# A hand-ordered two-part SSM kernel: another order of all engines' work, other buffer slots, and six groups of output stores issued by SyncE

## The chip, the cores and the metric

The kernel runs on one core of one Trainium2 chip. The metric is the device time of one execution in microseconds (us). A core has five engines that work side by side, each through its own list of instructions in order: TensorE (PE in the profile, its weight loads PEld), VectorE (DVE), ScalarE (ACT), GpSimd (POOL) and SyncE (SP). SP computes nothing; it issues transfers. POOL issues transfers as well. [...]

## The reference

Two independent parts share the launch, and their results are put side by side.

```python
def _A_ref(q, k, v, shift_k, ssm_k, ssm_D):          # S = 2048, D = 1024
    k_shift = sum of 4 shifted copies of k, each times a column of shift_k
    kv = k_shift * v
    y = irfft(rfft(kv padded to 2S) * rfft(ssm_k padded to 2S))[:S] + kv * ssm_D
    return q * y

def _B_ref(x, Lambda_re, Lambda_im, B_re, B_im, C_re, C_im, log_dt, Dskip):
    Lam_bar = exp(dt * Lam);  B_bar = ((Lam_bar - 1.0) / Lam)[:, None] * Bmat
    Bu = x @ B_bar.T                                  # complex
    for t in range(L): h = Lam_bar * h + Bu[t]        # complex state, kept for all t
    y = 2.0 * (hseq @ Cmat.T).real + x * Dskip
    return y

return concatenate([_A_ref(...), _B_ref(...)], axis=-1)
```

## The kernel before

The long string `ORDER` is the program: each word is one task, and words run from left to right, which fixes the order on every engine. A word is `task.args:slots`; `p0` to `p7` are the eight PSUM banks, `a..`, `b..`, `m..` and `w..` are numbered SBUF buffers. A task that takes a slot waits until the former user of the slot is done. Nothing is tiled by a loop; the order was written out by a planner beforehand.

Part B. `bl`/`cl` load blocks of B and C (256 KB each, SP), `bT`/`cT` transpose them on PE into PSUM (8 matmuls), `bc`/`cc` copy them to SBUF (ACT; `bc` for imaginary blocks 0 to 3 on DVE). `cx` loads blocks of C already transposed. `ld_par` loads four small vectors, `par_T`, `p32`, `exp1`, `dve2`, `tabA1`, `sin1`, `tabA2`, `par_rest`, `eo`, `z1`, `stt`, `z2` make the rotation tables out of them, `dd` the diagonal and the decay table. Then the sequence goes in 16 chunks of 128 steps: `x.i` loads the chunk, `U.i.jp` (32 matmuls) multiplies it with B, `ue` evicts; on DVE `r1`, `r2` rotate, `rc` adds the carry, `sc` scans, `cm`, `ca` make the next carry, `r3`, `r4` rotate back; `y.i.dh.part` multiplies with C, `ye` evicts and `yst` stores (chunk 15 is stored by `ye` itself from SP, L547).

Part A is a long convolution as a two-stage Fourier transform. `kp`, `vp` load k and v, `kvm`, `kv1`, `kv2`, `kva` make kv on DVE; `am` is its first stage (PE), `ae` evicts, `ast` stores to DRAM. `hl`, `hT`, `hc`, `hm`, `he`, `hst` do the same for the filter. Stage two, for 32 groups: `lw`, `lh`, `lk` load constants and both spectra, `sh`, `sk` multiply, `she`, `ske` evict, `sw` swaps halves by DMA, `pr` multiplies on DVE, `sa` goes back, `sae` evicts, `vst` stores. `vl` loads the result, `a3` is the last stage, `a3e` evicts, `qm` multiplies with q (loaded by `qp`), `op` stores four pieces (L786). `wb`, `wbe` broadcast the four taps, which `ld_w` loads.

`wm.n` is n matmuls on zeros whose result nobody reads. POOL issues `ld_w`, `ld_G`, `ld_F`, `ld_sd`, `ast`, `hst`, `vst`, `yst` and `op`; all loads and `sw` go through SP, which waits in order for slots and for one of eight semaphores: a ninth load is issued when the first has landed.

```python
spd = nc.sync.dma_start
gpd = nc.gpsimd.dma_start
```

Of the kernel before, what the change touches and what calls it, by code (L numbers as in the profile page):

```python
# [51 lines left out]
wbe.4 bT.0.1:p5 wbe.6 wb.0:p6 bc.0.1 wbe.5 wb.1:p7 wb.2:p0 wbe.0 wb.3:p1 wbe.2 wbe.3 ld_par wbe.7 wm.13:p3 bT.2.1:p3 wbe.1 bl.7.1:b5 bc.2.1 wm.3:p2
bT.0.0:p2 bl.2.0:b6 bc.0.0 bl.1.1:b7 wm.3:p5 bT.1.0:p5 bl.5.1:b8 bc.1.0 vp.0:a2 wm.14:p6 par_T:p6 p32 wm.5:p0 bT.7.1:p0 exp1 bc.7.1 dve2 wm.3:p1
bT.2.0:p1 x.0:b9 dve3 tabA1:a3a4a5a6 wm.3:p4 bT.1.1:p4 bc.2.0 bl.5.0:b10 wm.3:p7 bT.5.1:p7 exp2 cl.2.1:b0 bc.5.1 cl.2.0:b1 sm_pre sin1 kp.0 tabA2 sin0
bl.7.0:b2 bl.3.1:b3 wm.30:p3 bT.5.0:p3 bc.5.0 par_rest hl.2.1:a7 wm.3:p2 cT.2.1:p2 bl.4.1:b4 wm.3:p5 cT.2.0:p5 sin2 cc.2.1 bc.1.1 dd cc.2.0 wm.15:p6
# [798 lines left out]
```

## Time and profile before

| | us |
|---|---|
| median of 11 runs | 376.54 |
| lowest and highest run | 374.06, 378.57 |
| the profiled execution, own time | 377.71 |
| its span, first to last instruction | 375.8 |
| busy: PE, DVE, ACT, POOL | 356.9, 324.6, 278.3, 71.7 |
| mean granted TensorE clock | 0.986 |

A line of the timeline gives the start, the duration of a merged group, engine, source line, operation, output and inputs, the count, and in brackets the idle time before it and what ended it. A line of the windows gives the stretch, its length and the busy time (count) of PE, PEld, DVE, ACT and POOL, then the granted clock, the DMA share and GB/s.

### The profile page before, as it was taken

What the parts mean: (1) busy time and instruction counts of PE and PEld (TensorE: products, weight loads), DVE (VectorE), ACT (ScalarE), POOL (GpSimd) and SP (SyncE); (2) the same over time, 40 slices, a digit from 0 to 9 for tenths busy, and PEclk for the clock granted to TensorE, in tenths of its full rate; (3) what the DMA queues carried; (4) which work ended last, traced back from release to release, by engine and by line L of the source; (5) the groups of instructions that cost most, each with busy time, mean ns of one, the idle gap of its engine ahead of it and who ended that gap; (6) DMA issues with size and microseconds to landing.
All of it is one profiled execution on the core that took longest, in us unless ns stands there. A gap on an engine that the chain in (4) does not pass through costs nothing.

```text
span 375.8 us, 9490 instructions
## 1 busy us (share of the span) xinstructions
PE 356.9 (95%) x3821; PEld 250.1 (67%) x3851; DVE 324.6 (86%) x335; ACT 278.3 (74%) x519; POOL 71.7 (19%) x124
## 2 busy tenths in 40 slices
PE   7998699999999999999999999999999999999991
PEld 5777699996587787895855456457764445575640
DVE  2299989999999999999999999359999999159990
ACT  4599889989649875976558996788799975175541
POOL 4000003222331252221000110111010111124551
PEclk9999699999999999999999999999999999999997
DMA  8999999958989997589899899999797999799953
GB/s 214 275 295 284 334 255 274 262 181 222 263 280 198 331 232 219 164 292 340 272 270 275 281 280 328 289 268 331 198 329 216 281 271 329 259 399 402 326 150 95
DMA packets 61643, 101.14 MB, mean 269 GB/s; under 512 B 31536, under 2 KB 33872, under 8 KB 61599
## 3 DMA queue, kind: packets, MB, share of 16 engines
q1 hardware_dynamic: 51502, 67.13, 65.3%
q0 software_dynamic: 10096, 33.40, 26.3%
q8 instruction: 30, 0.49, 0.5%
q14 instruction: 15, 0.11, 0.1%
HBM read 52.27 MB, written 33.55 MB: 228 GB/s over the span
## 4 chain that ended last, share of the span: by engine, by line
PE 74%; ACT 9%; DMA 7%; DVE 4%; issue 2%; POOL 1%; POOLq 0%; ACTq 0%; DVEq 0%
PE ps_u L460 27%; PE ps_y L529 24%; PE ps_a L692 6%; PE ps_a L732 6%; PE ps_a L661 3%; DMA vv<-Vs 3%; DMA out_dram<-ot 3%; PE ps_t L424 2%; PE ps_y L534 2%; PE ps_t L641 2%; ACT hab L702 1%; ACT x L711 1%; PE ps_a L611 1%; DMA hk<-in_A_shift_k_dram 1%; POOL out_dram L786 1%
## 5 line engine op out<-in xcount | busy, mean ns | idle before, releaser
L460 PEld LDWEIGHTS <-BT 128*128 128x128 bf16 x2048 | 119.0, 99 | 9.7 <-issue 4.1
L460 PE MATMUL ps_u<-xT,BT 128*128 128x128 bf16 x2048 | 124.4, 221 | 0.9 <-DVE BT L435 0.6
L529 PE MATMUL ps_y<-CT,h 128*128 128x512 bf16 x488 | 122.8, 379 | 2.1 <-DVE h L488 0.8
L529 PEld LDWEIGHTS <-h 128*128 128x128 bf16 x512 | 45.1, 98 | 47.1 <-issue 1.9
L507 DVE TENSOR_TENSOR_SCAN h<-rtab,h 128x1024 bf16<-128x1024 f32 (+1 forms) x34 | 72.3, 2155 | 0.3
L462 ACT CAST u<-ps_u 128x512 bf16<-128x512 f32 x64 | 39.9, 635 | 31.4 <-PE ps_u L460 30.3
L545 ACT CAST yo<-ps_y 128x512 bf16<-128x512 f32 x32 | 19.5, 614 | 36.0 <-PE ps_y L529 35.7
L723 DVE TENSOR_TENSOR hab<-x,hab 128x2048 bf16<-128x2048 bf16 x32 | 37.9, 1218 | 4.5 <-ACT x L711 4.5
L479 DVE TENSOR_TENSOR mt<-u,Z 128x4096 bf16<-128x4096 bf16 x15 | 34.2, 2283 | 8.9 <-ACT u L462 8.9
L702 ACT CAST hab<-ps_a 128x512 bf16<-128x512 f32 x64 | 36.2, 666 | 4.2 <-PE ps_a L692 2.9
L488 DVE TENSOR_TENSOR h<-mt 128x2048 bf16<-128x2048 bf16 (+1 forms) x34 | 39.0, 1155 | 0.2
L741 ACT CAST vsb<-ps_a 128x512 bf16<-128x512 f32 x64 | 35.0, 650 | 5.7 <-PE ps_a L732 4.7
L711 ACT CAST x<-ps_a 128x512 bf16<-128x512 f32 x64 | 36.8, 683 | 1.5 <-DVE hab L723 0.8
L669 ACT CAST ysbh<-ps_a 128x512 bf16<-128x512 f32 x64 | 35.2, 660 | 0.2 <-PE ps_a L661 0.2
L479 DVE TENSOR_TENSOR mt<-h,Z 128x4096 bf16<-128x4096 bf16 x15 | 34.3, 2287 | 0.1
L622 ACT CAST ysb<-ps_a 128x512 bf16<-128x512 f32 x64 | 34.3, 674 | 0.0
L732 PE MATMUL ps_a<-hab,wts 128*128 128x512 bf16 x122 | 31.2, 379 | 0.2
L582 DVE TENSOR_TENSOR mt<-kring,wbc 128x4096 bf16<-128x4096 bf16 (+3 forms) x16 | 29.9, 1882 | 0.0
L627 POOL DMA_DIRECT2D Ys_kv<-ysb x16 | 11.5, 718 | 90.4 <-ACT ysb L622 90.4
L534 PE MATMUL ps_y<-Dd,xT 128*128 128x128 bf16 x128 | 28.1, 219 | 0.3 <-issue 0.2
L675 POOL DMA_DIRECT2D Ys_h<-ysbh x32 | 22.0, 693 | 30.2 <-ACT ysbh L669 29.4
L745 POOL DMA_DIRECT2D Vs<-vsb x16 | 8.5, 533 | 87.7 <-ACT vsb L741 87.7
(113 smaller groups left out, 403.4 us busy)
## 6 DMA issues: line engine op xcount, KB each, us to landing
Ys_kv<-ysb POOLq DMA_DIRECT2D x16, 512.0 KB, 4.7
Ys_h<-ysbh POOLq DMA_DIRECT2D x32, 256.0 KB, 4.9
l2h<-Ys_h SPq DMA_DIRECT2D x16, 512.0 KB, 4.8
hab<-hab SPq DMA_DIRECT2D x64, 128.0 KB, 4.5
l2k<-Ys_kv SPq DMA_DIRECT2D x16, 512.0 KB, 5.6
Vs<-vsb POOLq DMA_DIRECT2D x16, 512.0 KB, 5.1
vv<-Vs SPq DMA_DIRECT2D x16, 512.0 KB, 11.1
v<-in_A_v_dram SPq DMA_DIRECT2D x32, 128.0 KB, 4.9
```

What stands on the lines that cost most here:

```text
L460: nc.tensor.matmul(pu[:, w, jl, :], BT[:, 2 * jp + jl, w, d, :], xT[:, d, :], start=(d == 0), stop=(d == ND - 1))
L462: E["ue"] = lambda i, jp: nc.scalar.copy(st["u", i][:, :, 2 * jp:2 * jp + 2, :], st.pop(("pu", i, jp))[:])
L479: nc.vector.tensor_mul(m4[:].rearrange("p (a b) w -> p a (b w)", a=2), s_, win(Z, h))
L488: nc.vector.tensor_add(dst[:].rearrange("p a j t -> p a (j t)")[:, :, jw], mv[:, :, 0, jw], mv[:, :, 1, jw])
L507: nc.vector.tensor_tensor_scan(gf, rt1[:, jw], gf, 0.0, ALU.mult, ALU.add)
L529: nc.tensor.matmul(py[:], h[:, 1 - w, j, :], CT[:, j, w, dh * 512:(dh + 1) * 512], start=(j == 0 and w == 0), stop=(j == NJ - 1 and w == 1))
L534: nc.tensor.matmul(py[:, dl * P:(dl + 1) * P], st["xT", i][:, d, :], Dd[:, d, :], start=False, stop=False)
L669: nc.scalar.copy(st["yh", qd, n4][:, :, w, :], st.pop(("pa", qd, n4, w))[:].rearrange("p (c d) -> p c d", c=2))
L702: nc.scalar.copy(st["hab", g][:, 0, cols], pt[:])
L711: nc.scalar.copy(st["x16", g][:, w * 512:(w + 1) * 512], st.pop(("ps", "l2k", g, w))[:])
L723: nc.vector.tensor_mul(hab[:], st.pop(("x16", g))[:].unsqueeze(1).to_broadcast([P, 2, D]), hab[:])
L732: nc.tensor.matmul(pt[:], st["w", gq][:, gi, 1 + a, :], hab[:, a, w * 512:(w + 1) * 512], start=(a == 0), stop=(a == 1))
```

## The change

The words of `ORDER` are put in another order and given other slots. The tasks are the same but for `wm`: 205 zero matmuls in place of 194, at other places. `dd` stands after `stt` and no longer ahead of `kvm.0`; `kvm.2` stands ahead of `kva.0`; `vp.0` is issued behind `hl.0.0`. A new entry `late` of the settings names `op.3`, `yst.12`, `yst.13`, `yst.14`, `op.0` and `op.1`: these stores are issued by SP instead of POOL. `ldw` is 0, so `ld_w` stays on POOL.

```diff
-CFG = {'kr': 8, 'bdve': 4, 'K4': 13, 'kq': 2, 'tabct': 0, 'swsp': 1, 'th': (15,), 'actsw': ()}
+CFG = {'kr': 8, 'bdve': 4, 'K4': 13, 'kq': 2, 'tabct': 0, 'swsp': 1, 'ldw': 0, 'th': (15,), 'actsw': (), 'late': (('op', 3), ('yst', 12), ('yst', 13), ('yst', 14), ('op', 0), ('op', 1))}
...
-ld_w:a0a1 bl.6.1:b0 bl.0.1:b1 kp.-2 ld_G ld_sd ld_F bl.2.1:b2 bl.0.0:b3 wm.22:p0 bT.6.1:p0 wm.5:p1 wb.4:p1 bc.6.1 wb.5:p2 bl.1.0:b4 wb.6:p3 wb.7:p4
-wbe.4 bT.0.1:p5 wbe.6 wb.0:p6 bc.0.1 wbe.5 wb.1:p7 wb.2:p0 wbe.0 wb.3:p1 wbe.2 wbe.3 ld_par wbe.7 wm.13:p3 bT.2.1:p3 wbe.1 bl.7.1:b5 bc.2.1 wm.3:p2
-bT.0.0:p2 bl.2.0:b6 bc.0.0 bl.1.1:b7 wm.3:p5 bT.1.0:p5 bl.5.1:b8 bc.1.0 vp.0:a2 wm.14:p6 par_T:p6 p32 wm.5:p0 bT.7.1:p0 exp1 bc.7.1 dve2 wm.3:p1
-bT.2.0:p1 x.0:b9 dve3 tabA1:a3a4a5a6 wm.3:p4 bT.1.1:p4 bc.2.0 bl.5.0:b10 wm.3:p7 bT.5.1:p7 exp2 cl.2.1:b0 bc.5.1 cl.2.0:b1 sm_pre sin1 kp.0 tabA2 sin0
-bl.7.0:b2 bl.3.1:b3 wm.30:p3 bT.5.0:p3 bc.5.0 par_rest hl.2.1:a7 wm.3:p2 cT.2.1:p2 bl.4.1:b4 wm.3:p5 cT.2.0:p5 sin2 cc.2.1 bc.1.1 dd cc.2.0 wm.15:p6
-U.0.0:p6a8 kp.1 eo cl.1.1:b5 kvm.0:m0 bT.3.1:p0 cl.0.0:b6 bT.7.0:p1 bl.4.0:b7 hl.0.0:a9 wm.10:p7 bT.4.1:p7 bc.3.1 kvm.1:m1 bc.4.1 vp.1:a10 bc.7.0
-wm.23:p3 cT.1.1:p3 kv1.0 ue.0.0 wm.3:p4 cT.0.0:p4 bl.3.0:b8 cc.1.1 kv1.1 hl.0.1:a11 wm.3:p2 bT.4.0:p2 lw.2:w0 cc.0.0 kv2.0:b10 cl.3.1:b0 bc.4.0
-kv2.1:b1 kva.0 z1 kva.1 kvm.2:m0 cl.0.1:b3 wm.30:p5 am.0.0:p5p0p7p1 am.0.1:p6p3p4p2 bl.6.0:b2 x.1:b4 ae.0.0.2:a12 kvm.3:m1 hl.3.0:a0 ae.0.1.3
-bT.3.0:p7 lw.1:w1 ae.0.0.3 hT.0.0:p2 hl.3.1:a1 bc.3.0 hT.0.1:p1 hl.2.0:a2 cl.3.0:b5 hc.0.0:b6 U.0.1:p7 kv1.2 cx.5.0 hc.0.1:b7 hd.0 kv2.2:b10 lw.0:w2
-ae.0.1.2 cT.0.1:p2 kv1.3 ue.0.1 U.0.2:p1 lw.4:w3 ast.0.1 cc.0.1 kva.2 x.3:b1 kv2.3:b8 bT.6.0:p4 ue.0.2 stt cT.3.1:p7 bc.6.0 hT.0.2:p2 x.2:b3 hT.0.3:p1
-cc.3.1 U.0.3:p4 hl.1.0:a9 hc.0.2:b2 hc.0.3:b0 U.1.0:p7a11 cx.5.1 ue.0.3 kva.3 z2 r1.0:m0 hT.2.0:p2 hl.1.1:a10 ue.1.0 U.1.1:p1 ae.0.0.0:a12 ae.0.0.1
...
-y.11.0.1 she.28.0:a6 pr.31 sw.29 she.28.1 y.11.0.2 ske.29.0:b8 r3.12:m0 ske.29.1 y.11.0.3 sw.28 sa.27.0:p5 ye.11.0:b6 sa.27.1:p3 sae.27.0 pr.30
-sa.31.0:p6 sae.27.1 sa.31.1:p1 y.10.1.0:p2 qp.2:a3 cm.12 vst.13 r4.12 sa.30.0:p4 sa.30.1:p0 pr.29 sae.30.0:a11 y.10.1.1 sae.30.1 qp.7:a10 sae.31.0
-pr.28 y.10.1.2 sae.31.1 sa.29.0:p7 ca.12 vst.15 rc.13 sa.28.0:p5 sc.13.0 sa.28.1:p3 sae.28.0:a8 sa.29.1:p4 sae.28.1 y.12.0.0:p0 sae.29.0 sae.29.1
-y.12.0.1 qp.4:a7 sc.13.1 vst.14 U.14.0:p6a18 r3.13:m1 y.10.1.3 qp.5:a16 ue.14.0 y.12.0.2 ye.10.1 y.12.0.3 cm.13 yst.10 r4.13 y.12.1.0:p1 ye.12.0:b10
-ca.13 y.12.1.1 vl.6:a1a2 y.12.1.2 vl.3:a0a6 y.12.1.3 y.11.1.0:p5 ye.12.1 vl.7:a15a13 y.11.1.1 yst.12 vl.2:a11a12 y.11.1.2 y.11.1.3 U.14.1:p3 ye.11.1
-yst.11 a3.6.0:p7p4 ue.14.1 a3.6.1:p6p2 U.14.2:p0 a3e.6.0.0:a8 vl.4:a4a17 a3e.6.0.1 a3e.6.1.1 a3e.6.1.0 U.14.3:p1 ue.14.2 qm.6 op.6 a3.3.0:p5p3 ue.14.3
-a3.3.1:p7p4 y.13.0.0:p2 a3e.3.0.0:a1 vl.5:a2a14 r1.14:m0 a3e.3.1.1 a3e.3.1.0 U.15.0:p6a0 a3e.3.0.1 qm.3 a3.7.0:p0p1 ue.15.0 a3.7.1:p5p4 y.13.0.1
-a3e.7.0.0:a6 vl.0:a18a15 r2.14:a13 op.3 a3e.7.1.0 a3e.7.0.1 y.13.0.2 rc.14 a3e.7.1.1 sc.14.1 a3.2.0:p7p3 a3.2.1:p6p0 a3e.2.0.0:a9 y.13.0.3 vl.1:a11a12
-a3e.2.1.1 a3e.2.1.0 y.13.1.0:p5 sc.14.0 a3e.2.0.1 ye.13.0:b8 y.13.1.1 y.13.1.2 qm.2 y.13.1.3 U.15.1:p1 cm.14 r3.14:m1 ye.13.1 op.2 a3.4.0:p4p7 ue.15.1
-a3.4.1:p0p6 ca.14 U.15.2:p3 a3e.4.0.0:a8 qm.7 yst.13 a3e.4.1.1 a3e.4.1.0 r1.15.0:m0 qp.0:a5 a3e.4.0.1 a3.5.0:p2p5 ue.15.2 a3.5.1:p1p4 r4.14 U.15.3:p6
-a3e.5.0.0:a3 a3e.5.1.1 a3e.5.0.1 qm.4 a3e.5.1.0 y.14.0.0:p0 ue.15.3 r2.15.0:a4 r1.15.1 y.14.0.1 y.14.0.2 rc.15.0 qm.5 y.14.0.3 op.7 sc.15.1.0
-y.14.1.0:p7 ye.14.0:b3 r2.15.1 y.14.1.1 sc.15.0.0 op.4 y.14.1.2 qp.1:a17 rc.15.1 r3.15.0:m1 y.14.1.3 sc.15.0.1 a3.0.0:p3p2 ye.14.1 a3.0.1:p4p5
-a3.1.0:p1p6 a3e.0.0.0:a1 a3.1.1:p0p7 a3e.0.1.0 r4.15.0 a3e.0.0.1 sc.15.1.1 op.5 y.15.0.0:p3 a3e.0.1.1 a3e.1.0.0:a10 qm.0 y.15.0.1 a3e.1.1.0 a3e.1.1.1
-a3e.1.0.1 y.15.1.0:p4 r3.15.1 y.15.1.1 r4.15.1 qm.1 yst.14 y.15.0.2 y.15.0.3 y.15.1.2 ye.15.0:b4 op.0 y.15.1.3 ye.15.1 op.1 yst.15
...
+ld_w:a0a1 bl.0.1:b0 kp.-2 ld_G ld_F ld_sd bl.2.1:b1 bl.7.1:b2 bl.0.0:b3 wm.22:p0 bT.0.1:p0 bc.0.1 wm.23:p1 wb.4:p1 wb.0:p2 wbe.4 wb.5:p3 wb.6:p4 wbe.0
+wb.7:p5 wbe.6 wb.1:p6 wb.2:p7 wbe.7 wb.3:p0 wbe.2 bl.6.1:b4 ld_par wbe.3 wm.8:p1 bT.2.1:p1 wbe.1 wbe.5 bc.2.1 wm.3:p2 bT.7.1:p2 cl.0.0:b5 bl.5.0:b6
+bc.7.1 wm.3:p4 bT.0.0:p4 bl.1.1:b7 bc.0.0 bl.2.0:b8 wm.7:p5 bT.6.1:p5 bc.6.1 kp.0 wm.6:p7 par_T:p7 p32 wm.5:p0 cT.0.0:p0 exp1 cc.0.0 dve2 wm.3:p6
+bT.5.0:p6 x.0:b9 dve3 tabA1:a2a3a4a5 exp2 wm.3:p3 bT.1.1:p3 bc.5.0 bl.1.0:b10 wm.3:p1 bT.2.0:p1 bl.7.0:b0 bl.4.1:b1 bc.2.0 sm_pre sin1 kp.1 tabA2 sin0
+bl.5.1:b2 bl.3.1:b3 wm.30:p2 bT.1.0:p2 par_rest bc.1.0 cl.2.0:b4 wm.3:p4 bT.7.0:p4 hl.0.0:a6 sin2 wm.3:p5 bT.4.1:p5 bc.4.1 kvm.0:m0 bc.7.0 vp.0:a7 eo
+wm.23:p7 bT.5.1:p7 bc.1.1 wm.3:p0 bT.3.1:p0 cl.1.1:b5 kvm.1:m1 bl.4.0:b6 U.0.0:p6a8 cl.2.1:b7 hl.2.1:a9 cT.2.0:p1 bc.3.1 kv1.1 ue.0.0 vp.1:a10 bc.5.1
+kv1.0 wm.21:p2 cT.1.1:p2 cc.2.0 kv2.1:b8 wm.3:p5 bT.4.0:p5 bl.3.0:b10 kv2.0:b0 cc.1.1 hl.0.1:a11 wm.3:p4 cT.2.1:p4 kvm.2:m1 cl.0.1:b1 bc.4.0 bl.6.0:b2
+cc.2.1 z1 kva.0 kva.1 hl.1.0:a12 kvm.3:m0 wm.30:p3 am.0.0:p3p0p6p7 x.1:b3 am.0.1:p1p2p5p4 ae.0.0.0:a0 x.2:b4 ae.0.1.0 kv1.2 bT.3.0:p3 ae.0.0.1
+hT.0.0:p1 hl.3.1:a1 bc.3.0 hT.0.1:p0 cl.3.1:b5 kv1.3 hl.2.0:a7 hc.0.0:b6 U.0.1:p3 lw.1:w0 kv2.2:b7 cx.6.0 hc.0.1:b0 kv2.3:b8 kva.2 ae.0.1.1 cT.0.1:p1
+lw.0:w1 ue.0.1 hd.0 bT.6.0:p0 lw.2:w2 kva.3 ast.0.0 cc.0.1 U.0.2:p2 stt bc.6.0 cl.3.0:b10 ae.0.0.2:a10 hm.0.1.0:p3 U.0.3:p1 ae.0.0.3 x.3:b1 ae.0.1.3
+ae.0.1.2 ue.0.2 lw.4:w3 hT.0.2:p0 ast.0.1 ue.0.3 hT.0.3:p6 dd hc.0.2:b2 cT.3.1:p7 U.1.0:p4a6 hc.0.3:b5 hl.3.0:a11 z2 r1.0:m1 hl.1.1:a0 hT.2.0:p5
...
+sa.28.0:p2 ye.10.0:b2 sa.28.1:p6 sae.28.0:a13 y.10.1.0:p1 sae.28.1 pr.26 qp.7:a9 y.10.1.1 cm.11 r4.11 y.10.1.2 qp.3:a15 y.10.1.3 pr.29 sa.26.0:p5
+ye.10.1 sa.26.1:p4 ca.11 rc.12 sae.26.0:a5 sa.29.0:p3 sc.12.0 yst.10 sae.26.1 sa.29.1:p2 sae.27.0 y.11.0.0:p6 sae.27.1 sae.29.0 y.11.0.1 vst.13
+qp.6:a10 sae.29.1 sc.12.1 y.11.0.2 vst.14 y.11.0.3 y.11.1.0:p1 cm.12 r3.12:m1 ye.11.0:b5 y.11.1.1 y.11.1.2 ca.12 r4.12 y.11.1.3 rc.13 U.14.0:p5a14
+sc.13.1 ye.11.1 yst.11 vl.7:a0a11 y.12.0.0:p4 ue.14.0 vl.4:a2a3 sc.13.0 y.12.0.1 vl.6:a18a12 y.12.0.2 vl.5:a6a5 y.12.0.3 r3.13:m0 U.14.1:p0 ye.12.0:b7
+cm.13 r4.13 U.14.2:p7 ue.14.1 ca.13 a3.7.0:p3p2 ue.14.2 a3.7.1:p6p1 y.13.0.0:p5 a3e.7.0.0:a8 vl.2:a13a0 a3e.7.0.1 a3e.7.1.1 a3.4.0:p4p0 a3.4.1:p7p3
+a3e.7.1.0 y.13.0.1 vl.3:a11a2 a3e.4.0.0:a3 qm.7 a3e.4.0.1 y.13.0.2 a3e.4.1.0 a3e.4.1.1 U.14.3:p2 op.7 qm.4 a3.6.0:p1p6 ue.14.3 a3.6.1:p4p0 op.4
+y.12.1.0:p7 a3e.6.0.0:a9 vl.0:a1a18 r1.14:m1 a3e.6.0.1 a3e.6.1.0 y.12.1.1 a3e.6.1.1 y.12.1.2 qm.6 y.12.1.3 r2.14:a12 a3.5.0:p3p2 ye.12.1 a3.5.1:p1p6
+y.13.0.3 a3e.5.0.0:a14 vl.1:a10a7 rc.14 a3e.5.0.1 sc.14.1 y.13.1.0:p4 a3e.5.1.0 ye.13.0:b8 a3e.5.1.1 a3.2.0:p0p7 a3.2.1:p3p2 a3e.2.0.0:a6 y.13.1.1
+op.6 qm.5 a3e.2.1.0 a3e.2.1.1 y.13.1.2 a3e.2.0.1 sc.14.0 y.13.1.3 U.15.0:p1a5 ye.13.1 qp.0:a13 qm.2 U.15.1:p5 op.5 ue.15.0 r3.14:m0 a3.3.0:p6p0
+ue.15.1 a3.3.1:p3p2 U.15.2:p7 a3e.3.0.0:a0 cm.14 r1.15.0:m1 a3e.3.1.1 a3e.3.0.1 r4.14 a3e.3.1.0 U.15.3:p4 ue.15.2 op.2 r2.15.0:a8 ca.14 qm.3
+y.14.0.0:p1 ue.15.3 rc.15.0 r1.15.1 y.14.0.1 sc.15.1.0 a3.0.0:p5p6 a3.0.1:p2p0 a3e.0.0.0:a17 y.14.0.2 a3e.0.1.0 sc.15.0.0 qp.1:a16 op.3 a3e.0.1.1
+y.14.0.3 a3e.0.0.1 r2.15.1 y.14.1.0:p3 ye.14.0:b3 r3.15.0:m0 y.14.1.1 rc.15.1 r4.15.0 y.14.1.2 sc.15.1.1 yst.12 y.14.1.3 yst.13 sc.15.0.1 y.15.0.0:p7
+ye.14.1 qm.0 yst.14 a3.1.0:p4p5 a3.1.1:p2p0 a3e.1.0.0:a3 y.15.0.1 a3e.1.1.1 r3.15.1 a3e.1.0.1 y.15.1.0:p6 a3e.1.1.0 op.0 r4.15.1 y.15.1.1 qm.1
+y.15.0.2 y.15.0.3 op.1 y.15.1.2 ye.15.0:b9 y.15.1.3 ye.15.1 yst.15
...
-            gpd(st["wraw"][m][0:1, :], A_shift_k.rearrange("(o d) j -> o (d j)", o=2)[m:m + 1, :])
+            (nc.scalar.dma_start if c["ldw"] else gpd)(st["wraw"][m][0:1, :], A_shift_k.rearrange("(o d) j -> o (d j)", o=2)[m:m + 1, :])
...
-            gpd(out_b[i * T:(i + 1) * T, :], yo[:])
+            (spd if ("yst", i) in c["late"] else gpd)(out_b[i * T:(i + 1) * T, :], yo[:])
...
+        f = spd if ("op", u) in c["late"] else gpd
         for b in range(4):
-            gpd(oar[b, :, 2 * u:2 * u + 2, :], t_[32 * b:32 * b + 32, :, :])
+            f(oar[b, :, 2 * u:2 * u + 2, :], t_[32 * b:32 * b + 32, :, :])
```

## The prediction

> **What bounds the kernel now.** I read the page first, then the windows, the timelines of PE and DVE up to 60 us, the landings, and the last ten microseconds.
>
> ```profile
> span 375.8 us, 9490 instructions
> PE 356.9 (95%) x3821; PEld 250.1 (67%) x3851; DVE 324.6 (86%) x335; ACT 278.3 (74%) x519; POOL 71.7 (19%) x124
> ```
>
> ```profile
> 30.00:40.00 10.00, 6.62 (x110) 5.69 (x111) 10.00 (x11) 10.00 (x20) 0.00 (x0) 1.00 1.16 293
> 160.00:180.00 20.00, 19.95 (x256) 14.76 (x255) 20.00 (x16) 13.76 (x28) 3.83 (x6) 1.00 0.92 303
> 360.00:365.00 5.00, 4.41 (x25) 2.18 (x27) 4.97 (x6) 3.19 (x7) 1.94 (x5) 1.00 0.31 92
> ```
>
> From 50 to 360 us PE is busy over 99%, at the full clock. A busy PE need not be a PE at its peak, so I checked by counting: merged groups give 1.79 us for a `U` word, 0.98 or 0.86 for a `y` part, 0.22 for `sh`/`sk`, 0.43 for `sa`; all work behind `U.0.2` sums to about 316 us, and 50 to 368 us is 318. So the middle can hardly be shortened by any order. What an order can still move is the head, where PE runs fillers and waits, and the end.
>
> The head:
>
> ```profile
> 4.62 0.74 PE L252 MATMUL warm<-wz 128*128 128x128 bf16 x5
> 6.61 1.88 PE L410 MATMUL ps_a<-hk,ones 1*128 1x512 bf16 x4 [1.26 <-DMA hk<-in_A_shift_k_dram]
> 11.21 1.57 PE L252 MATMUL warm<-wz 128*128 128x128 bf16 x13
> 17.60 0.17 PE L264 MATMUL ps_t<-ident,praw 32*128 32x32 bf16 x1
> 34.47 1.84 PE L252 MATMUL warm<-wz 128*128 128x128 bf16 x30
> 39.37 1.14 PE L611 MATMUL ps_a<-acc,F1t 32*64 32x512 bf16 x16 [3.06 <-DVE acc L600]
> 44.18 3.55 PE L460 MATMUL ps_u<-xT,BT 128*128 128x128 bf16 x32
> 48.01 1.95 PE L460 MATMUL ps_u<-xT,BT 128*128 128x128 bf16 x32
> ```
>
> Thirteen zero matmuls take 1.57 us at 11 us, thirty take 1.84 at 34: until about 17 us PE runs at half rate. It does so again for one stretch after the gap of 3.06 us:
>
> ```profile
> 40.70:47.50 6.80, 5.83 (x56) 5.83 (x56) 6.80 (x7) 5.22 (x8) 0.74 (x1) 0.50 1.01 351
> ```
>
> The gap waits for `kva.1` at the end of a DVE chain that starts with `par_T` at 17.6 and has no idle time of note:
>
> ```profile
> 28.15 1.39 DVE L382 TENSOR_SCALAR Dd<-ident,p 128x128 bf16<-128x128 bf16 x8
> 39.73 4.50 DVE L582 TENSOR_TENSOR mt<-kring,wbc 128x4096 bf16<-128x4096 bf16 x2
> ```
>
> The vectors that `par_T` needs had landed at 11.6 us by the landing events. It starts 6 us later because PE is in order, and slow.
>
> The end:
>
> ```profile
> L849 POOLq DRAIN x3: 46/108/7623, 367.3 to 375.5; - x3
> L849 SPq DRAIN x3: 7/7/7, 372.0 to 375.2; - x3
> ```
>
> The last matmul ends at 368.2, the last store (SP, issued 368.9) lands at 371.6, and SP reaches its closing barrier at 372.1. POOL's drain, begun at 367.3 behind its last `op.1` store, lasts 7.62 us, to 375.0, and all engines wait for it.
>
> **The change, part by part.** The sum is made against the profiled execution's own 377.71 us, which stands 1.2 above the median.
>
> *Start.* Before, five zero matmuls leave PE idle 1.26 us until the taps land at 6.6. Now 23 stand there: from 4.62 at half rate (0.107 each, from 1.57/13 less its tail) they end at 7.1. PE is busy from 1.13 to 7.1 without a gap over 0.2 us. When does the clock rise? The row: from 6.61 PE was 98% busy and still needed 10.2 us. [...] much of that stretch is `wb`, with one row of weights; the rising clock followed the first stretch of full matmuls. [...] by the row (10.2 us from 1.13) at 11.3. [...]
>
> *`par_T`.* From 7.1 at full rate: 8 `wb` x 0.22 = 1.8, 27 zero matmuls x 0.056 = 1.5, four transposes x 0.6 with their issue gaps = 2.4: 12.8 us, against a landing that cannot move (2,050 KB are ahead in both orders, 11.6 us). By the row: 15.2. At half rate throughout: 17.9. Before: 17.6.
>
> *DVE chain.* 17.6 to 39.8 was 22.2 us. `dd` leaves it (28.15 to 30.05, 1.9 us), `kvm.2` enters (half of 4.50, 2.25): 22.5. So `kva.1` ends at 35.3. Would its data be there? `vp.0` is moved past nine loads and `kp.0`, `kp.1`; 6,914 KB have then gone through SP's queue, and in the trace that byte count had landed at 30.2 us. It lands in time for `kva.0` at 34. `dd` itself costs its 1.9 us behind `stt`, ahead of `r1.0`.
>
> *ACT.* Its copies ahead of `am.0` are the same number (11), `eo` 4.7 us starts at `par_rest` (`par_T` + 9.9 = 22.7), then six evictions, 5.0, then `z1` 2.85. `cl.2.1` lands at 32.2 by bytes, so `cc.2.1` ends at 33.6 and `z1` at 36.5. The first `ae` frees a bank at 37.0 (41.5 before).
>
> *To `U.0.1`.* The PE tasks ahead of `am.0` are the same set. `bl.3.0` (8,962 KB) lands at 37.7, `hl.0.1` at 39.0, so `bT.3.0` and `hT.0.0`, `hT.0.1` end at 40.0 and `U.0.1` at 41.9, where it ended at 47.7. That is -5.8, and landings, not PE, set it. `r1.0` on DVE: `kva.1` 35.3, then `kvm.3`, two `kv1`, two `kv2`, two `kva`, `hd`, `stt`, `dd` = 2.25+2.3+1.3+1.3+0.2+4.2+1.9 = 13.5, so 48.8 for 54.8: -6.0. Both engines move together, and what PE and DVE still have to do is the same.
>
> *Middle.* Counted from `U.0.1` and `r1.0`, the PE work ahead of each `y.i.0.0` exceeds the DVE work up to `r4.i` by at least 7.9 us before and 7.1 after, of which 7 us is the offset between the two starts. Tight in both orders, broken in neither. In stage two, loads stand closer to their use. PE work between the word and the use: `lw.8` 5.1 before, 4.0 after; `lw.10` 8.3, 4.2; `lk.4` 6.8, 5.1; `lh.2` 14.7, 5.8; `sw.18` 19.9, 6.5. The row that prices it:
>
> ```profile
> wts<-a_c_W SPq DMA_DIRECT2D x16, 192.0 KB, 4.2
> ```
>
> SP can issue ahead of the word, so a lead near the landing time need not stall; bounds are 0 and 8 such loads x 1 us. I take +1.0.
>
> *Tail.* `r1.14` to `r4.15.1` is about 29 us on DVE; behind `U.14.3` PE has 34 us, 4 of them after the half that needs `r4.15.1`. It fits as before (a wait of 0.76); 0. The last `vst` is followed by 17 us of PE work up to the first `a3` (15.6 before), and the first `vl` landed 5.1 us after its issue: covered.
>
> *Stores on SP.* POOL loses 4+3+4+4 issues of 0.54-0.58 us, SP gains 15 of about 0.42. Nothing loads behind them: `qp.1` is ahead of `op.3`. `op.1` waits on `qm.1` 2.5 us ahead of the last matmul, four issues take 1.7, so `ye.15.0`'s store is late by some 0.4 us and `ye.15.1`'s, which ends the program, not at all. [...] By the drain rows: POOL's last store is then `op.2`, over 10 us ahead of the end, its drain is over, and the barrier falls to SP's 372.1: 375.0 - 372.1 = -2.9. I take the row.
>
> Sum: -5.8 - 2.9 + 1.0 = -7.7; 377.71 becomes 370.0. Off the median 376.54 it is 368.8, with the assumption that a typical run has the same head.
>
> **The rivals.**
>
> *The clock stays half to 11 or 17 us.* For it: the 10.2 us above. Then `par_T` is at 15.2 or 17.9, and in the latter case `U.0.0` also waits 3 us for `bc.1.1`, now behind `kvm.0`. The head gives 3 to 0 us: 371.6 to 374.6. Chance 0.22.
>
> *The clock falls again.* PE waits about 2 us between `am.0.1` and `bT.3.0`, then 0.5 for `hl.0.1`; a gap of 3.06 halved it before, for 6.8 us with 5.8 busy, 2.9 lost. -7.7 + 2.9 = -4.8: 371.7. Chance 0.15.
>
> *The drain does not depend on the last POOL store.* Then 371.7. Chance 0.08.
>
> *Slower: stage two runs into late loads.* Place: the `lw`, `lh`, `lk` and `sw` with leads under 6.5 us, 150 to 290 us. SP stands in order, and a swap that waits for its eviction (`SPq L717` waited 23.8 us in all) holds the constants behind it; PE then idles. The present order has almost no such gap, so each is a new loss. To beat the 8.7 us of head and end it takes over 1.1 us at each of eight loads; slower by 0.5% needs 1.3. Price at 2 us each: +16 - 8.7, 384. Chance 0.10, of which half stays within or under no change.
>
> **How the numbers follow.** The forecast has 0.45, and ends at 366 to 370.5 (without the stalls and with PE's last gaps closed, 366.5). About 0.5%, 1.9 us, can be told from no change here. Faster by that is below 374.7: the forecast, the fallen clock, the drain, nearly all of the slow start and some of the late loads: 0.87. Same 0.08, slower 0.05. The range 365.5 to 374.6 takes in all but the late loads and the edges.
>
> **What would show it.** Right: thirty-odd zero matmuls at 0.06 us each before 11 us; `par_T` near 13; `am.0` near 35; the second `U` group ending near 42 at clock 1.00; POOL's long drain starting well before 365 and the end within 4 us of the last store's issue. Wrong: `par_T` at 17 or later; clock 0.50 in a window after 30 us; PE idle for `wts`, `l2h`, `l2k` or `hab`; a closing barrier that still waits for POOL.

## The result, and the profile after

| | before | after |
|---|---|---|
| median, us | 376.94 (47 runs in all) | 371.84 (12 runs) |
| lowest and highest run | 372.69, 378.74 | 370.05, 377.75 |
| the profiled execution, own time | 377.71 | 371.35 |
| its span | 375.8 | 369.5 |

The ratio of after to before is 0.9881, 95% interval 0.9854 to 0.9909: faster by 1.2%, or 5.1 us on the medians, where 7.7 were forecast. The forecast of 368.8 us was 3.0 too low; the time lies inside its range. In some executions of nine of these kernels (before, after, e1 to e4, e6 to e8) the time is 1.5% or more above the fastest: the medians include them and the ratios do not, and the profile of e7 is of one such (380.58 us), of which only the first 45 us are used.

The page of after, first its span and busy time, then the granted clock in 40 slices:

```profile
span 369.5 us, 9523 instructions
PE 351.5 (95%) x3829; PEld 245.9 (67%) x3862; DVE 325.7 (88%) x335; ACT 277.7 (75%) x519; POOL 64.1 (17%) x109
PEclk9998999999999999999999999999999999999999
```

PE's timeline in the head of after:

```profile
4.56 1.45 PE L252 MATMUL warm<-wz 128*128 128x128 bf16 x23
6.66 1.90 PE L410 MATMUL ps_a<-hk,ones 1*128 1x512 bf16 x8 [0.66 <-DMA hk<-in_A_shift_k_dram]
12.88 0.17 PE L264 MATMUL ps_t<-ident,praw 32*128 32x32 bf16 x1
31.70 0.98 PE L424 MATMUL ps_t<-ident,ld 128*128 128x128 bf16 x8 [3.14 <-DMA ld<-in_B_C_im_dram]
37.13 0.64 PE L611 MATMUL ps_a<-acc,F1t 32*64 32x512 bf16 x16
39.83 0.61 PE L424 MATMUL ps_t<-ident,ld 128*128 128x128 bf16 x8 [2.05 <-ACT ysb L622]
41.71 1.95 PE L460 MATMUL ps_u<-xT,BT 128*128 128x128 bf16 x32 [0.25 <-ACT BT L435]
```

Twenty-three zero matmuls in 1.45 us are 0.06 each: the clock was full from 4.5 us. (Ahead of its first change the profile records no clock, and its column says 1.00; that PE ran at half rate there is read from zero matmuls of about 0.11 us.) `par_T` is at 12.88 (forecast 12.8, before 17.60), `am.0` at 37.13 (forecast near 35, before 39.37), and the second `U` group ends at 43.66 (forecast 41.9, before 47.73). New is the wait of 3.14 us for `cl.1.1`.

DVE ends `kva.1` at 35.94 (forecast 35.3). ACT idles for the transposes that stand behind that wait, and its first `ae`, from 39.19 on, frees the bank for `bT.3.0` only at 39.8 (forecast 37.0). DVE's timeline, then ACT's:

```profile
34.65 1.29 DVE L600 TENSOR_TENSOR acc<-acc,v 128x1024 bf16<-128x1024 bf16 x2
```

```profile
32.72 1.01 ACT L444 COPY CT<-ps_t 128x1024 bf16<-128x1024 bf16 x1 [1.32 <-PE ps_t L424]
39.19 1.56 ACT L622 CAST ysb<-ps_a 128x512 bf16<-128x512 f32 x3
```

The windows of after. The second line is the stretch behind that wait, and its clock is 0.50; the third has the one gap in stage two; the fourth is PE's end:

```profile
27.00:31.80 4.80, 1.66 (x30) 1.49 (x28) 4.80 (x5) 4.41 (x11) 0.00 (x0) 1.00 0.95 272
31.80:35.21 3.41, 3.30 (x30) 2.97 (x30) 3.41 (x4) 2.02 (x2) 0.00 (x0) 0.50 1.04 248
280.00:300.00 20.00, 18.29 (x91) 8.41 (x92) 18.57 (x15) 17.29 (x36) 1.12 (x3) 1.00 0.83 212
360.00:365.00 5.00, 4.95 (x27) 2.38 (x26) 2.54 (x3) 1.66 (x4) 0.00 (x0) 1.00 0.71 178
```

The gap in PE's timeline, and the closing line of the program (engine queue, operation, count, ns min/median/max, first and last start):

```profile
292.28 0.39 PE L692 MATMUL ps_a<-l2k,wts 128*128 128x512 bf16 x1 [1.61 <-DMA wts<-a_c_W]
```

```profile
L850 POOLq DRAIN  x3: 46/99/9469, 345.5 to 369.2; - x3
L850 SPq DRAIN  x3: 7/7/7, 368.6 to 368.9; - x3
```

PE waits for `lw.14`, issued at 286.45 and landed at 292.24. POOL's long drain starts at 345.5 and is over at 355, long before SP is done at 368.7. The last matmul ends at 365.66, the program 3.80 us later (before 7.52).

In this pair of profiles the head gives -4.07 (end of `U.0.1`), the stretch from there to the last matmul +1.49, and the end -3.72: -6.3. That is 1.2 us more than the medians moved, and the experiments show why one pair of profiles is not enough.

### The profile page after: what moved, and what is told of

It reads as the page before. It is cut to its first block, busy times and chain, and to the rows that moved or that the text cites. A ratio compares the mean times of both kernels' runs of the same rounds, so it can differ in the third digit from the quotient of the medians.

```text
span 369.5 us, 9523 instructions
## 1 busy us (share of the span) xinstructions
PE 351.5 (95%) x3829; PEld 245.9 (67%) x3862; DVE 325.7 (88%) x335; ACT 277.7 (75%) x519; POOL 64.1 (17%) x109
## 4 chain that ended last, share of the span: by engine, by line
PE 81%; DMA 8%; ACT 5%; SPq 3%; issue 2%; ACTq 0%
PE ps_u L460 29%; PE ps_y L529 28%; PE ps_a L692 7%; PE ps_a L732 6%; PE ps_a L661 4%; DMA ld<-in_B_B_im_dram 3%; DMA ld<-in_B_C_im_dram 2%; PE ps_y L534 2%; DMA xT<-in_B_x_dram 2%; DMA wts<-a_c_W 2%; PE ps_t L424 1%; SPq L567 1%; PE ps_t L641 1%; PE ps_a L765 1%; PE ps_a L611 1%
## 5 line engine op out<-in xcount | busy, mean ns | idle before, releaser
L460 PEld LDWEIGHTS <-BT 128*128 128x128 bf16 x2048 | 117.1, 98 | 8.1 <-issue 3.1
L460 PE MATMUL ps_u<-xT,BT 128*128 128x128 bf16 x2048 | 121.4, 219 | 0.6 <-ACT BT L435 0.2
L711 ACT CAST x<-ps_a 128x512 bf16<-128x512 f32 x64 | 35.9, 644 | 2.0 <-PE ps_a L692 2.0
L424 PE MATMUL ps_t<-ident,ld 128*128 128x128 bf16 x192 | 15.9, 232 | 7.8 <-DMA ld<-in_B_C_im_dram 3.1
```

Source lines behind the costliest of these rows:

```text
L460: nc.tensor.matmul(pu[:, w, jl, :], BT[:, 2 * jp + jl, w, d, :], xT[:, d, :], start=(d == 0), stop=(d == ND - 1))
L711: nc.scalar.copy(st["x16", g][:, w * 512:(w + 1) * 512], st.pop(("ps", "l2k", g, w))[:])
```

## Experiments

Twelve runs follow, one of them of after itself, each timed side by side with the kernel before. One theory stood behind them: the time is the sum of three stretches, up to the end of `U.0.1`, from there to the last matmul (PE is busy throughout), and behind it. Worked out from the records of each profile (PE's gaps are those over 0.12 us between its matmuls and weight loads behind `U.0.1`; each row but for its median is of one execution):

```
                                      par_T  U.0.1   to last   gaps   last matmul  median
                                             ends    matmul    in it  to the end   us
before                                17.60  47.73   320.51    0.89   7.52         376.94
e1  before + stores on SP             16.14  46.32   321.37    1.17   4.41         373.04
e12 before + stores on SP + fillers   14.77  47.55   320.50    0.89   4.42         373.20
e5  before + fillers                  13.27  43.37   325.21    4.70   7.51         377.03
after                                 12.88  43.66   322.00    1.76   3.80         371.84
e11 after, again                      15.07  43.58   322.53    2.26   3.79         371.03
e2  after, all stores on POOL         14.89  43.33   321.62    1.02   6.97         374.37
e3  after, op.1 on POOL               14.57  43.22   323.63    2.71   6.07         375.17
e4  after, four earlier on POOL       16.09  44.43   323.73    2.40   4.46         373.41
e6  after, 5 fillers                  16.43  44.33   325.79    4.05   3.81         372.84
e8  after, lw.14 early                14.80  43.24   323.07    2.27   3.80         372.18
e9  after, more fillers               19.03  47.70   322.25    1.36   3.80         375.48
e10 e9 + lw.14 early + hl.0.0 late    18.80  47.42   321.15    0.78   3.81         375.39
```

### The end: who issues the last stores

**e1.** The order before; three stores go to SP. `op.0` and `op.1` move ahead of `ye.15.0`, so that the last half store is not behind them.

```diff
- 'actsw': ()}
+ 'actsw': (), 'late': (('yst', 14), ('op', 0), ('op', 1))}
- y.15.1.2 ye.15.0:b4 op.0 y.15.1.3 ye.15.1 op.1 yst.15
+ y.15.1.2 op.0 op.1 ye.15.0:b4 y.15.1.3 ye.15.1 yst.15
```

> The kernel before with its last three stores (yst.14, op.0, op.1: nine DMAs) issued by SyncE, nothing else. Theory (the end is POOL's closing drain, which runs about 7 us past POOL's last store): POOL's last store is then op.5 at about 358, its drain is over by about 367, and the end stands 3.8 us behind the last matmul as in the kernel after, not 7.5: -3.7 in the profile, about 372.8 to 373.6 us, ratio 0.990 to 0.993. Rival (the end waits for the last landing, whoever issues it): 376.5, ratio 1.000. Rival (SyncE's stores get in one another's way): the last half store is issued 1 to 2 us later than 368.9 and half of the gain is lost.

Measured: 373.04 us, ratio 0.9908 (0.9873 to 0.9942): -3.5 us. The closing line of e1:

```profile
L850 POOLq DRAIN  x3: 46/99/7219, 356.9 to 371.8; - x3
L850 SPq DRAIN  x3: 7/7/35, 370.9 to 371.3; - x3
```

POOL's drain is over at 364.2; the barrier comes when SP is done, 4.41 us behind the last matmul. The last half store was issued 0.65 us behind the last matmul's end, 368.34 against 367.69, exactly as in after, so SP's stores are not in one another's way; the 0.6 above after's 3.80 lies partly in SP's closing waits and partly behind the barrier. This single part brings over two thirds of the whole gain (0.9% of 1.2 to 1.4%).

**e2, e3, e4.** The order after; `late` loses entries.

```diff
- 'late': (('op', 3), ('yst', 12), ('yst', 13), ('yst', 14), ('op', 0), ('op', 1))
+ 'late': ()                                                        # e2
+ 'late': (('op', 3), ('yst', 12), ('yst', 13), ('yst', 14), ('op', 0))   # e3
+ 'late': (('op', 0), ('op', 1))                                    # e4
```

> The kernel after with all its stores but the last two halves back on POOL (24 DMAs move from SyncE to POOL), order unchanged. Theory: POOL's last store is issued at about 364.8, its drain ends about 7 us later at 371.7 and the end is 372.4 instead of 369.4: +3.0, about 374.9 us. Rival (a cost per store on POOL against SyncE): the same here, so this run alone does not tell them apart; the next two do. Rival (the end waits for landings only): 371.9.

> The kernel after with op.1 alone (four DMAs, the last that POOL would issue) back on POOL. Theory (only the time of POOL's last store counts): all of the loss of the run with everything on POOL, +3.0, about 374.9 us. Rival (a cost per store, 4 of 24): +0.5, about 372.4 us.

> The kernel after with op.3, yst.12, yst.13 and yst.14 (seven DMAs) back on POOL, op.0 and op.1 left on SyncE. Theory: POOL's last store is yst.14 at about 358.3, its drain ends at about 366 to 368, before SyncE's closing wait (368.7), and nothing is lost: 371.9 us (at most +0.5). Rival (a cost per store, 7 of 24): +0.9, about 372.8 us.

Measured: e2 374.37 us (ratio 0.9958, 0.9929 to 0.9987), e3 375.17 (0.9945, 0.9921 to 0.9969), e4 373.41 (0.9892, 0.9854 to 0.9930). The closing lines of e2, e3 and e4 in turn:

```profile
L850 POOLq DRAIN  x3: 46/108/7627, 363.5 to 371.7; - x3
```

```profile
L850 POOLq DRAIN  x3: 46/99/6728, 365.4 to 372.6; - x3
```

```profile
L850 POOLq DRAIN  x3: 46/99/6763, 361.0 to 372.4; - x3
```

`late` holds fifteen DMAs (the 24 expected were a miscount). Four DMAs on POOL (e3) cost as much as fifteen (e2), within the intervals: the end stands 6.1 and 7.0 us behind the last matmul, because a drain of 6.7 and 7.6 us begins at POOL's last store. In e4 the last of seven is issued 7.1 us ahead of the last matmul's end, the drain is over at 367.8, within SP's own waits, and the end stands at 4.46, as in e1. So what counts is when POOL's last store is issued, not how many it issues. e4's median stands 1.5 above the expected 371.9, but its ratio is only 0.0011 above after's, well inside its interval, and its profile has the latest head of those with an unchanged head (44.43), which its edit does not touch. e2 is also the new order without the change of stores: -2.2 us on the medians, 0.4% by the ratio, whose interval does not reach 1.

### The start: clock and fillers

**e5, e6.** The fillers ahead of the first `wb`, put into the order before, and taken out of the order after.

```diff
- wm.22:p0 bT.6.1:p0 wm.5:p1 wb.4:p1
+ wm.22:p0 bT.6.1:p0 wm.23:p1 wb.4:p1     # e5, on before
- bc.0.1 wm.23:p1 wb.4:p1
+ bc.0.1 wm.5:p1 wb.4:p1                  # e6, on after
```

> The kernel before with 23 zero matmuls in place of 5 ahead of the first wb, nothing else. Theory now (profiles of the runs so far: the clock changes only at the edges of a fixed grid of 3.41 us, rises after a stretch of full matmuls, and falls again in the stretch of one-row wb matmuls): the clock rises at the first edge after 4.5, may fall for one or two periods in the wb stretch, par_T comes 0 to 2 us earlier than 17.6, and the end gains 0 to 2 us: 374.6 to 376.6 us. Forecast on record (the fillers bring the early clock, and with it the head's 5.8 us): par_T near 13, about 371 us. Rival (the head hangs on the order of loads and tables, not on the clock): 376.6, ratio 1.000.

> The kernel after with 5 zero matmuls in place of 23 ahead of the first wb, nothing else. Theory now: PE idles 1.3 us more ahead of the taps, in most executions the clock is full only at 13 to 17, par_T at 15 to 17, and since loads and DVE's order hold the head as well, the end loses 0.5 to 2 us: 372.4 to 373.9 us. Forecast on record: the early clock is worth the head's gain, +4 to +5.8: 376 to 377.5 us. Rival (the order alone): 371.9.

Measured: e5 377.03 us, ratio 1.0012 (0.9984 to 1.0040): nothing. e6 372.84 us, ratio 0.9893 (0.9855 to 0.9931): +1.0 against after's median, inside both intervals, so the fillers' worth in the order after is not shown. Yet in the profile of e5 the fillers do what the prediction said. PE's timeline of e5:

```profile
13.27 0.17 PE L264 MATMUL ps_t<-ident,praw 32*128 32x32 bf16 x1
30.02 0.62 PE L424 MATMUL ps_t<-ident,ld 128*128 128x128 bf16 x8 [3.50 <-DMA ld<-in_B_B_im_dram]
36.50 0.64 PE L611 MATMUL ps_a<-acc,F1t 32*64 32x512 bf16 x16
41.42 1.95 PE L460 MATMUL ps_u<-xT,BT 128*128 128x128 bf16 x32
```

`par_T` is 4.3 us earlier than in before's profile and `U.0.1` ends 4.4 earlier, at full clock. This execution is not typical: its mean granted clock is 0.996, that of the other thirteen of e5 0.981 to 0.992, so the clock fell in those, and what their heads won is not known. In this one, what was won is gone at 91 us, by the waits of e5 (line, waited for, us in total, times, longest):

```profile
PE ps_y L529 <- DMA CT<-in_B_C_im_dram: 1.9, 1, 1.9
PE ps_a L661 <- ACT ysb L622: 1.8, 1, 1.8
```

The first is at 91.5, for the last transposed load of C; the second at 70.6. In this profile that load landed at 91.4 us, in before's at 76.1, 15 us ahead of its use. It was issued at 84.3 in e5 (before 69.4): SP stood up to 6.3 us at the issue of one of the transposed loads ahead of it, up to 3.3 in before. What held SP was not settled. By the medians, the fillers alone do not shorten the order before.

In the order after, the head gains without an early `par_T` too. PE's `par_T` in e1 and in e6:

```profile
16.14 0.17 PE L264 MATMUL ps_t<-ident,praw 32*128 32x32 bf16 x1
```

```profile
16.43 0.17 PE L264 MATMUL ps_t<-ident,praw 32*128 32x32 bf16 x1
```

`U.0.1` ends at 46.32 in e1, and at 44.33 in e6 with its later `par_T`: 2.0 us that an early start does not explain. In e6 the clock stayed full up to there (its mean is 0.999); in e1 it was half for 6.83 us (`PEclk` of 37.2 to 46.5 us: 6).

**e7.** One load that is not used before 40 us, moved behind three that are.

```diff
- cl.2.0:b4 wm.3:p4 bT.7.0:p4 hl.0.0:a6 sin2 ... cl.1.1:b5 ... bl.4.0:b6 U.0.0:p6a8 cl.2.1:b7 hl.2.1:a9
+ cl.2.0:b4 wm.3:p4 bT.7.0:p4 sin2 ... cl.1.1:b5 ... bl.4.0:b6 U.0.0:p6a8 cl.2.1:b7 hl.0.0:a6 hl.2.1:a9
```

> The kernel after with one load moved: the 0.5 MB hl.0.0 (landed at 29.4, not used before 40) goes behind cl.1.1, bl.4.0 and cl.2.1 on SyncE. Theory: cl.1.1 lands at about 28.8 instead of 31.7, PE's wait of 3.1 us at 31.7 falls below 0.5, the clock does not fall at 31.8, am.0 comes at about 36 (kva.1 on DVE ends at 35.9) instead of 37.1: -0.8 to -1.2, about 370.7 to 371.1 us. Rival (DVE is busy all through 27 to 37 us and holds am.0, and then hl.0.0 is late for hT.0.0 or hl.0.1 for hT.0.1): no gain, 371.9, with PE waiting for kva.1 or hk instead.

Measured: 371.99 us, ratio 0.9891 (0.9842 to 0.9940): no gain; the rival holds. PE's timeline of e7:

```profile
36.84 1.58 PE L611 MATMUL ps_a<-acc,F1t 32*64 32x512 bf16 x16 [2.92 <-DVE acc L600]
```

The wait for `cl.1.1` is gone, and 2.92 us for DVE's `kva.1` stand there instead: PE has about 3 us to spare ahead of `am.0` wherever they are spent. `par_T` stands at 14.53 in e7; with one as early as in after's profile, where PE's wait for `cl.1.1` did put `am.0` behind `kva.1`, the move was not seen.

**e11, e12.** After itself, and the order before with both simple parts (e1's and e5's edits together).

> The kernel after itself, for a second profile of it and for its times beside the others of this call: 371.5 to 372.2 us; the second U group starts between 41.2 and 42.5 as the edges of the clock's periods fall; PE waits 0 to 1.6 us for lw.14 near 292.

> The kernel before with both simple parts of the change, the last three stores on SyncE (as e1) and 23 zero matmuls ahead of the first wb (as e5), its order otherwise as it was. Theory (the fillers bring nothing, the stores all of it, and the rest of the new order about 1 us): as e1, 372.6 to 373.4 us, with par_T at 13 to 16, the second U group at about 41.5, and PE waiting 1 to 2 us each at about 69 or 90 us. Rival (the two gains add up and the order is worth nothing by itself): 370.5 to 371.5 us.

Measured: e11 371.03 us, ratio 0.9864 (0.9820 to 0.9908); e12 373.20, ratio 0.9904 (0.9870 to 0.9938). The fillers add nothing that shows to e1 here either. PE's timeline of e12, and its windows:

```profile
31.32 1.04 PE L424 MATMUL ps_t<-ident,ld 128*128 128x128 bf16 x8 [3.49 <-DMA ld<-in_B_B_im_dram]
```

```profile
26.55:29.97 3.42, 1.28 (x23) 1.11 (x20) 3.42 (x5) 3.42 (x13) 0.00 (x0) 1.00 1.05 274
29.97:36.79 6.82, 5.36 (x48) 5.04 (x49) 6.82 (x8) 4.14 (x7) 0.00 (x0) 0.50 0.97 266
```

The order before waits 3.5 us for a block of B that stands too late in SP's queue for an early `par_T`, as in e5; here the clock fell on it, and `U.0.1` ended at 47.55, no earlier than in before. In the order after, that wait is not there; in after's own profile one of 3.14 us for a block of C is, the clock fell on it too, and `U.0.1` still ended at 43.66. That the new order is what makes the early start usable fits these profiles, but no run shows it by itself. With fillers and the last stores on SP in both, e11 is 2.2 us below e12, but the two intervals overlap. The same kernel after, in another execution (PE's timeline and windows of e11):

```profile
12.11 1.01 PE L424 MATMUL ps_t<-ident,ld 128*128 128x128 bf16 x8
15.07 0.17 PE L264 MATMUL ps_t<-ident,praw 32*128 32x32 bf16 x1
37.37 1.34 PE L611 MATMUL ps_a<-acc,F1t 32*64 32x512 bf16 x16 [2.06 <-DVE acc L600]
```

```profile
7.45:10.86 3.41, 3.30 (x29) 1.89 (x29) 0.27 (x1) 3.00 (x7) 0.00 (x0) 1.00 1.09 362
10.86:14.28 3.42, 3.31 (x30) 2.98 (x30) 0.42 (x1) 2.94 (x5) 0.00 (x0) 0.50 0.86 272
```

Here the clock rose at 7.45 and fell again at 10.86, behind a period full of `wb`: transposes took 1.01 us at 12 us for 0.61 in after's first profile, and `par_T` came at 15.07, 2.2 later.

**e9, e10.** Full matmuls between the `wb` parts, to hold the clock, without and with both moved loads.

```diff
- wm.23:p1 wb.4:p1 wb.0:p2 wbe.4 wb.5:p3 wb.6:p4 ...
+ wm.36:p1 wb.4:p1 wm.5:p2 wb.0:p2 wbe.4 wm.5:p3 wb.5:p3 wm.5:p4 wb.6:p4 ...
- wm.8:p1 bT.2.1:p1 ... wm.7:p5 bT.6.1:p5 ... wm.6:p7 par_T:p7
+ bT.2.1:p1 ... wm.3:p5 bT.6.1:p5 ... wm.3:p7 par_T:p7
```

> The kernel after with 36 zero matmuls in place of 23 ahead of the first wb and 5 ahead of each of the other seven wb parts (and 12 fewer behind them), so that no 3.41-us period holds mostly one-row matmuls. Theory (the head's end is held by loads and DVE, and what PE gains there is taken back at about 69 us, by ACT's ysb, and at about 90 us, by the transposed loads of CT): the clock is full from 8 us at the latest and does not fall in the wb stretch, par_T comes at 13.5 to 14.5, the second U group starts at 41 to 42 as before, 371.3 to 372.3 us. Rival (forecast on record: an early clock is worth microseconds at the end): 369.5 to 371 us.

> The kernel after with the held clock of e9 and both moved loads (hl.0.0 behind cl.2.1, lw.14 ahead of sw.21): a try at a kernel that beats both. Theory: the second U group starts at about 40.5, but a wait of 1 to 2 us each at 69 (ACT's ysb) or 90 us (CT) takes most of it back; the wait for lw.14 is gone: 370.8 to 371.8 us. Rival (nothing stands behind the head): 368.5 to 370 us.

Measured: e9 375.48 us, ratio 0.9974 (0.9954 to 0.9995); e10 375.39, ratio 0.9969 (0.9953 to 0.9986). Both theory and rival miss: 3.6 us slower than after. The windows of e9, then its timeline:

```profile
8.28:11.69 3.41, 3.19 (x29) 1.65 (x27) 0.00 (x0) 1.75 (x3) 0.00 (x0) 1.00 1.01 328
11.69:18.52 6.83, 6.55 (x50) 4.76 (x47) 0.69 (x1) 4.08 (x6) 0.00 (x0) 0.50 1.00 257
```

```profile
19.03 0.17 PE L264 MATMUL ps_t<-ident,praw 32*128 32x32 bf16 x1
41.49 1.22 PE L611 MATMUL ps_a<-acc,F1t 32*64 32x512 bf16 x16 [2.93 <-DVE acc L600]
```

Five fillers a part were too few: the clock fell all the same, now for 6.83 us, and the fillers ran at half rate in front of `par_T`. The failed edit still shows the step behind it. `par_T` is 4.0 later than in e11, `am.0` 4.1, the end of `U.0.1` 4.1, the median 3.6 to 4.5 (against after's two medians). In the order after a late start costs about its whole delay.

### Stage two: the late weights

**e8.** The load that PE waited for, ahead of two swaps.

```diff
- ske.20.0:b9 sw.31 ske.20.1 y.9.0.1 ske.21.1 sw.21 ... sw.20 sae.25.0 sae.25.1 y.9.0.3 lw.14:w0 vst.12
+ ske.20.0:b9 sw.31 lw.14:w0 ske.20.1 y.9.0.1 ske.21.1 sw.21 ... sw.20 sae.25.0 sae.25.1 y.9.0.3 vst.12
```

> The kernel after with one load moved: lw.14 (the weights that PE waits for 1.6 us at 292.3) goes ahead of the copies sw.21 and sw.20 on SyncE, right behind sw.31. Theory: it is issued at about 283 instead of 286.5, lands at about 288.5 and is there when sk.28 wants it at 290.7; sw.20's second half lands 0.6 later at 291.4: -1.0 to -1.6, about 370.3 to 370.9 us. Rival (the copies that now stand behind it are late for sa.21 or sa.20, or vst's stores hold the queue): PE waits for hab instead, 371.4 to 371.9.

Measured: 372.18 us, ratio 0.9879 (0.9832 to 0.9926): no gain, as the rival says. In the profile the load was issued at 284.86, landed at 288.60, and PE's wait there was gone. The waits of e8 show others:

```profile
PE ps_a L692 <- DMA l2k<-Ys_kv: 1.0, 1, 1.0
PE ps_a L732 <- DVE hab L723: 0.7, 2, 0.6
```

Since the waits for other inputs vary between executions (0 to 1.5 us in all for `hab` in the profiles of the order after), the gaps sum to 2.27 us, as much as in e11. No kernel that ran beats after by more than its interval; e10, made to, is slower.

## Why the prediction was right, and where it was off

**End: forecast -2.9, measured -3.5 (e1) and -3.7 (profiles).** The step held: POOL's drain, not the landing of the data, held the program. In before the last store had landed at 371.6, the drain ran to 375.0, and with the last three stores on SP e1 was 3.5 us shorter. The term was sized as the gap between POOL's 375.0 and SP's 372.1. In after SP itself also ends sooner behind the last matmul, 3.0 us instead of 3.8.

**`par_T`: forecast 12.8, measured 12.88 in after's own profile, but 14.57 to 16.09 in the other five of the same head (e11, e2, e3, e4, e8).** This is the step that failed, "From 7.1 at full rate: 8 `wb` x 0.22". No view of before showed a full rate from 7.1: there PE was 98% busy for the 10.2 us ahead of the rise at 16.80. The early rise was right (4.49 in after, 7.45 in e11), the full rate afterwards was not: the clock fell again in the `wb` stretch in five of six (`PEclk` of the second fortieth of the span, 9.2 to 18.5 us: 7 in e4, 8 in e11, e2, e3 and e8, 9 in after). That after's own profile hit the forecast was luck: its mean granted clock is 0.995, and of after's twelve executions only three have 0.994 or more; the other nine have 0.986 to 0.991, where e11's profile has 0.990 with two stretches of 3.41 us at half rate and e4's 0.986 with three. The rival of a second fall was named, at another place, and the 371.84 measured stands at its 371.7. A clock of 0.50 after 30 us and PE idle for `wts` or `hab`, named as signs of being wrong, both came. Nor had before's profile the head of a typical run, as the sum assumed: in e1, with the same head, `par_T` came at 16.14 and `U.0.1` ended 1.4 us earlier. Hence 6.3 us between the two profiles and 5.1 between the medians.

**DVE chain: forecast 22.5 us from `par_T` to `kva.1`.** It was 22.75 to 22.77 in e11, e2, e3, e4, e6 and e8, whatever the clock had done, and 23.06 in after's first profile, where `par_T` was earliest. This step held.

**`U.0.1`: forecast -5.8 (41.9).** In after's order it ended at 43.2 to 44.4 in five profiles with the unchanged head (after, e11, e2, e3, e4; e8 lies among them); in before's at 46.3 to 47.7 (before, e1). Mean against mean, 43.6 and 47.0, is -3.4: -2.2 by `par_T` (14.7 for 16.9), +0.6 from there to `kva.1`, and -1.8 from `kva.1` to the end of the group (6.1 for 7.9), where PE runs at half clock for 6.83 us in before and e1 and for at most 3.41 here. The forecast had -4.8, +0.3 and -1.3, so `par_T` is the term that was mis-sized.

"Landings, not PE, set it" did not hold in most of these: in e11, e2 and e4 the end is `par_T` + 22.3 (to `am.0`) + 6.0 to 6.2. But in after's own profile, where `par_T` came as forecast, a landing that the sum does not list cost as much: PE's wait of 3.14 us for `cl.1.1` and the half clock behind it put `am.0` 1.2 behind `kva.1` and left ACT idle for 2.0 us ahead of its first `ae`, and the group ended at 43.66, no earlier than in e11. `r1.0` on DVE moved with PE, as forecast: 50.7 for 54.1 in the same means.

**Middle: forecast +1.0, measured about +1.8** (means 322.7 of the same five, which lie between 321.6 and 323.7, and 320.9 of the two). The kind was right, loads and swaps of stage two with less lead, but not the names: `lw.14`, at 0 to 1.6 us, was not among those listed, and waits for `hab`, up to 1.5 us in a profile, were another part. Gaps explain some 1.0 of the 1.8; the remainder was not traced.

The three measured terms, -3.4 + 1.8 - 3.7 = -5.3, stand against -5.1 of the medians. The new order with its fillers, without the stores, is worth 2.2 us by e2's median and 1.6 by its ratio, and 1.2 by the difference between e1 and after, 2.0 with e11: the head's 3.4 less what the middle takes back. What `dd`, `kvm.2`, `vp.0` and the new slots each bring was not tried.

**The slower case** needed over a microsecond at each of eight loads; the profiles of the order after with the unchanged head show gaps of 1.0 to 2.7 us in all.

## What to carry to other kernels

Look at what the closing barrier waits for before tuning the last microseconds of work: here POOL's drain took 6.7 to 9.5 us and SP's 7 to 35 ns, so POOL's last transfer had to stand well ahead of the end, and the last store task alone, four DMAs, was enough to lose most of the gain (375.17 in e3 for 371.84). A head that is filled with dummy work to raise the clock has to be judged over several profiles: in e11 a period of 3.41 us that was busy for 3.30, but for 1.49 without `wb`, ended with the clock falling. The mean granted clock of each execution helps to tell how typical a profile is. And an earlier start is worth only what the loads behind it can follow (in the order before PE then waited 3.5 us for a block of B, in e5 and e12), so try the part alone in the old order before crediting it.

## What the runs showed of the hardware

**The clock's periods.** In the profiles of before and after, the stretches between changes of the granted clock, from its first rise to its fall at the end, are 23.89, 6.83 and 324.27 us in before and 27.31, 3.41 and 334.51 us in after: 7, 2, 95, 8, 1 and 98 times 3.413. The edges lie elsewhere in each of three executions: the first rise is at 16.80 in before, 4.49 in after and 7.45 in e11. PE's busy time in single periods, in us, with all matmuls and without `wb` (periods ahead of the first rise are counted back from it, and the clock there is read from the matmuls' own durations):

```
                          busy   without wb   clock   at its end
before   6.56 to  9.97    3.36      1.03      half    stayed half
before   9.97 to 13.38    3.35      2.12      half    stayed half
before  13.38 to 16.80    3.31      3.31      half    rose
before  33.86 to 37.28    2.39      2.39      full    stayed full
before  37.28 to 40.69    1.03      1.03      full    fell
before  40.69 to 44.10    2.44      2.44      half    stayed half
before  44.10 to 47.52    3.42      3.42      half    rose
after    1.08 to  4.49    3.21      3.21      half    rose
after    4.49 to  7.90    2.75      1.52      full    stayed full
after   28.38 to 31.80    0.28      0.28      full    fell
after   31.80 to 35.21    3.30      3.30      half    rose
after   38.62 to 42.04    1.97      1.97      full    stayed full
e9       8.28 to 11.69    3.19      1.96      full    fell
e11      7.45 to 10.86    3.30      1.49      full    fell
e12     26.55 to 29.97    1.28      1.28      full    fell
```

Where the clock rose, PE had been busy for 3.21 to 3.42 us without `wb`. With `wb`, which has one row of weights, counted as busy, the lines do not sort: before's period from 6.56 was busy for 3.36 us, 1.03 of them without `wb`, and the clock stayed half; e11's from 7.45 was busy for 3.30, 1.49 of them without `wb`, and the clock fell. That it stayed full in after behind 1.52 and 1.97 us, and fell in e9 behind 1.96, is not explained.

**POOL's drain.** It took 6.7 to 7.6 us where it began at 357 to 368 us (before, e1 to e4, e12), and 8.7 to 9.5 where at 345 to 350 (after, e6, e8 to e11); why it differs was not looked into. SP's took 7 to 35 ns. The end of the program hung on POOL's drain for 2.3 us in e3, 3.2 in e2 and 3.7 in before, by the ends behind the last matmul against after's 3.80.
